# Chunk-selected attention and a top-1 expert layer on one core: a new written order, the last tile's down product in two column halves, and a first activation of one column

## The chip, the core and the metric

The kernel runs on one core of a Trainium2 chip. The metric is the device time of one execution in microseconds (us). TensorE is called PE, VectorE DVE, ScalarE ACT, GpSimd POOL and SyncE SP.

## The reference

```python
# attention: 4 batches, 8 heads, 768 positions, head size 64, float32
k_min, k_max = min and max of k over chunks of 32 positions            # 24 chunks
ub   = sum_d max(q_d * k_min_d, q_d * k_max_d)                         # bound for each query and chunk
sel  = the 6 chunks of highest ub among those not after the query's
attn = softmax(where(sel and causal, q @ k.T / 8, -1e9));  x = attn @ v   # x: 3072 tokens x 512
# expert layer: 8 experts, 512 -> 1024 -> 512, one expert for each token
p = softmax(x @ w_gate);  e = argmax(p)
out[token] = p[e] * (relu(x[token] @ w1[e]) @ w2[e])
```

## The kernel before, in words

The attention works on 16 pairs of heads, numbered 0 to 15, four to a batch. The two heads of a pair lie in the upper and lower 64 partitions. The routed tokens then go through the experts in 26 tiles, numbered 0 to 25, of 128 rows: tiles 0 to 9 hold tokens of the first three batches, so they can start before the last batch has been routed; tiles 10 to 25 wait for it. Tiles 20 to 25 share 128 rows between two experts.

All work is written as steps, such as `kt.12`: the step `kt` for pair 12. One long string, `ORDER`, lists every step of the program, and each engine and each queue runs its own steps in the order in which the string has them. An engine waits at a step until the data and the buffer are there, and everything behind that step on the same engine waits with it. The steps that matter here:

- `lk lq lv` load k, q and v of a pair (SP queue, L192, L194). `w.0` to `w.31` load and convert a quarter of one expert's weights each, 512 KB (POOL queue, L182).
- `kt qt` transpose k and q on PE (L208, tiles pk and pq). `kr0 kr1` reduce pk to chunk maxima and minima on DVE (L214). `qR qN` write the positive and negative part of q (ACT, L226), `kc qc` copy k and q to bf16 (ACT, L218 and L230).
- `ub` multiplies the bounds (PE, L242, tile pc). `sel1` to `selt` choose the chunks on DVE and end in the mask mt.
- `sc0` to `sc5` are six blocks of scores (PE, L288 and, for the mask, L296, tile ps), `ex0` to `ex5` their exponentials (ACT, L304), `cm` the causal corrections (POOL, L311), `av` the products with v (PE, L324, tiles ob and oa), `ac` the sums over blocks for the denominator (DVE, L335).
- `ocB ocA` copy the attention output from PSUM (ACT). `sm gt` (PE) and `uc` (ACT, L368) and `ut` (PE, tile pc, L199) and `rcp lgt` (DVE, L386 to L400) form denominators and gate logits. `xt` (PE, L199, tile px) and `xr` (DVE, L422) write the token rows. `lga` adds logits over pairs on POOL (L408).
- `ra` to `rp` route one batch, nearly all on DVE; `rx` is their one exponential, on ACT (L445), and `rk` their one product, on PE. `s0` to `s5` scatter a batch's rows to DRAM from POOL. `tA tB tC` compute on DVE the tables that say which rows and which expert a tile has.
- For a tile, `x` reads 128 token rows from DRAM through a DMA transpose (SP queue, L743), `U` is the product with w1 (PE, L783), `Rl` the relu (ACT, L792), `H` a DMA transpose of the hidden values (SP queue, L802), `D` the product with w2 (PE, L809), `Y` the scaling by the gate (ACT, L816), `O` the scatter to the output (POOL, L820). `g` fetches the tokens' gates and row numbers (ACT or POOL queue). `z` are matmuls on zeros at the start, `sp` pauses on POOL.

The PSUM tiles pk, pq, pc, ps, px and ph share three buffers. Which of the three a tile gets is fixed when the program is built, from the order in which the string gives and frees them; at run time PE waits until the last reader of the tile that had the buffer before is done. The hidden values h have two buffers, so `Rl` of a tile waits for the `H` of the tile two before.

The weights of all experts lie in two tiles, and a product picks its expert by a register; so the first `U` waits for all sixteen loads of w1, and the first `D` for all sixteen of w2. A `U` or `D` of a whole tile is 8 matmuls of 512 columns, or 16 where each half of the rows has its own expert; these come in pairs that use 64 columns of the array each.

## Time and profile before

| what | value |
|---|---|
| median of 3 runs | 308.94 us (308.81 to 317.49) |
| the profiled execution | 305.6 us, its span 303.7 us |
| PE busy | 285.2 us (94%) |
| DVE busy | 197.0 us (65%); next to nothing after 250 us |
| ACT, POOL busy | 189.3 us (62%), 159.5 us (53%) |
| granted TensorE clock | 0.998 of full speed |

Up to about 205 us the span is attention, with the first expert tile begun at 197.8 us; from there to 298 us it is the experts. An idle time in brackets stands behind an instruction that its engine began late, with what ended the wait; "issue" means that the profile shows no release. A matmul's end is modelled and reaches a little past the start of the next, so the distance from start to start is the better measure of what a group costs.

### The profile page before, as it was taken

Reading aid. Unit: us, or ns where it says so; the run is one execution under the profiler, and the core shown is the slowest. Engines: PE = TensorE matmul, PEld = TensorE weight load, DVE = VectorE, ACT = ScalarE, POOL = GpSimd, SP = SyncE. Lnnn points to the kernel's source line nnn. Section 1 sums busy time; section 2 is a strip of 40 time slices with the busy share of each in tenths; the row PEclk is TensorE's granted clock in tenths of the full one; section 3 lists DMA queues with packets and bytes.
Section 4 is the critical chain, followed back from the end, with each engine's and each line's share of the span. In section 5 each row is a group of like instructions: output and inputs, shape, how many; then the busy total and the mean of one; then the engine's idle time right before and its main releaser. Section 6 shows DMA issues by size and latency. Waiting matters only on the chain.

```text
span 303.7 us, 8579 instructions
## 1 busy us (share of the span) xinstructions
PE 285.2 (94%) x3095; PEld 145.3 (48%) x3105; DVE 197.0 (65%) x613; ACT 189.3 (62%) x266; POOL 159.5 (53%) x245
## 2 busy tenths in 40 slices
...
GB/s 152 201 193 202 201 190 210 177 204 167 208 163 160 191 208 211 149 229 171 189 244 204 159 205 194 106 167 149 224 224 176 208 150 210 235 191 228 139 172 77
DMA packets 132587, 56.51 MB, mean 186 GB/s; under 512 B 121915, under 2 KB 121917, under 8 KB 132544
## 3 DMA queue, kind: packets, MB, share of 16 engines
...
q14 instruction: 15, 0.12, 0.1%
HBM read 53.26 MB, written 9.99 MB: 208 GB/s over the span
## 4 chain that ended last, share of the span: by engine, by line
PE 61%; DVE 9%; issue 9%; POOL 6%; DMA 5%; ACT 4%; SPq 3%; POOLq 1%; DVEq 0%; ACTq 0%
PE oa L324 16%; PE ph L783 8%; PE py L809 6%; PE ps L288 6%; DVE Pa L335 5%; PE ps L296 5%; PE pc L242 4%; PE pc L352 4%; POOL out_dram L820 3%; PE ob L324 3%; PE pc L362 2%; DMA KQ<-xg 2%; PE pq L208 2%; PE px L199 2%; DMA x_early<-xs_dram 2%
## 5 line engine op out<-in xcount | busy, mean ns | idle before, releaser
L304 ACT ACTIVATE Pa<-ps 128x1024 f32<-128x1024 f32 x64 | 65.1, 1024 | 15.2 <-PE ps L296 10.0
L335 DVE TENSOR_TENSOR Pa<-Pa 128x1024 f32<-128x1024 f32 (+2 forms) x64 | 64.5, 1008 | 6.9 <-PE oa L324 2.2
L324 PE MATMUL oa<-Pa,v 128*64 128x512 f32 (+2 forms) x320 | 64.3, 518 | 0.0
L311 POOL TENSOR_SCALAR_AFFINE_SELECT Pa<-Pa 128x256 f32<-128x256 f32 x48 | 25.1, 538 | 50.0 <-ACT Pa L304 47.4
L809 PE MATMUL py<-w_all,hT 128*128 (+1 forms) x251 | 46.9, 379 | 1.5 <-issue 1.2
L792 ACT ACTIVATE h<-ph 128x1024 bf16<-128x1024 f32 (+1 forms) x27 | 26.5, 990 | 31.5 <-DMA hT<-h 12.7
L288 PE MATMUL ps<-KQ 64*128 64x512 bf16 (+3 forms) x256 | 37.3, 307 | 1.3 <-ACT Pa L304 0.6
L820 POOL DMA_INDIRECT out_dram<-y,tag_all x26 | 25.7, 989 | 22.9 <-ACT y L816 18.6
L500 POOL DMA_INDIRECT xs_dram<-xrow,sli x24 | 27.8, 1156 | 13.4 <-issue 4.8
L296 PE MATMUL ps<-mt,IND 64*128 64x256 bf16 (+4 forms) x512 | 34.4, 225 | 0.2 <-DVE mt L272 0.2
L809 PEld LDWEIGHTS <-hT 128*128 128x128 bf16 (+1 forms) x256 | 20.8, 102 | 26.0 <-issue 3.3
L816 ACT ACTIVATE y<-py,tag_all 128x512 f32<-128x512 f32 x26 | 17.6, 687 | 21.3 <-PE py L809 19.5
L214 DVE TENSOR_REDUCE KK<-pk 128x24 f32<-128x768 f32 x32 | 29.2, 943 | 1.3 <-PE pk L208 1.2
L324 PEld LDWEIGHTS oa<-Pa,v 128*64 128x64 f32 x320 | 19.4, 136 | 19.8 <-issue 14.7
L783 PE MATMUL ph<-w_all,x_early 128*128 (+1 forms) x125 | 25.3, 379 | 3.0 <-DMA x_early<-xs_dram 2.4
L288 PEld LDWEIGHTS <-KQ 64*128 64x128 bf16 x256 | 13.2, 94 | 28.9 <-issue 28.4
L296 PEld LDWEIGHTS <-IND 64*128 64x128 bf16 x512 | 23.0, 94 | 7.5 <-issue 0.4
L311 POOL TENSOR_SCALAR_AFFINE_SELECT Pb<-Pb 128x256 f32<-128x256 f32 x32 | 20.7, 672 | 9.7 <-ACT Pb L304 8.1
L182 POOL DMA_DIRECT2D w_all<-in_moe_w_dram x32 | 23.9, 748 | 0.1
L752 DVE TENSOR_TENSOR tag_all<-tag_all,inv_i 128x1 int32<-128x1 int32 x10 | 1.5, 158 | 31.8 <-DMA tag_all<-xs_dram 28.5
L783 PE MATMUL ph<-w_all,KQ 128*128 (+1 forms) x127 | 21.9, 380 | 0.1
L226 ACT ACTIVATE qN<-pq 128x576 f32<-128x576 f32 x16 | 10.4, 652 | 15.4 <-PE pq L208 15.4
...
## 6 DMA issues: line engine op xcount, KB each, us to landing
...
hT<-h SPq DMA_TRANSPOSE x27
out_dram<-y,tag_all POOLq DMA_INDIRECT x26
xs_dram<-xrow,sli POOLq DMA_INDIRECT x24
tag_all<-xs_dram ACTq DMA_DIRECT2D x20, 1.0 KB
```

The costliest lines, as they stand in the source:

```text
L214: nc.vector.tensor_reduce(KK[i % 2][:, n, 0:NCH], st[i]["pk"].rearrange("p (c w) -> p c w", w=CH), AX.X, ALU.max if n == 0 else ALU.min, n ...
L288: nc.tensor.matmul(ps[:, hd, ds(c0, w)], lhsT=kc_[r, ts(kb_, 128)], rhs=qc_[r, ds(q0, w)], start=True, stop=False, skip_group_check=True)
L296: nc.tensor.matmul(o[:, :, c, :], lhsT=IND[c][r, ts(kb_, 128)], rhs=mt[r, ds(j0, n), :], start=False, stop=True, skip_group_check=True)
L304: nc.scalar.activation(P[:], st[i][f"ps{u}"][:, :, 0:w], AF.Exp)
L311: nc.gpsimd.affine_select(out=pd, in_=pd, pattern=[[0, 2], [1, 128]], compare_op=ALU.is_ge, fill=0.0, base=0, channel_multiplier=-1)
L324: nc.tensor.matmul(po[64 * hd:64 * hd + 64, ds(q0 - o0, w)], lhsT=vt[:, kb_, hd, :], rhs=P[:, hd, ds(c0, w)], start=(u <= 1 and n == 0), s ...
L335: nc.vector.tensor_tensor(a[:, :, ds(q0_, w)], a[:, :, ds(q0_, w)], P[:, :, ds(c0, w)], ALU.add)
L500: d = nc.gpsimd.indirect_dma_start(out=xs_dram[:], out_offset=bass.IndirectOffsetOnAxis(ap=sli[:, u:u + 1], axis=0), in_=bst[b]["xrow"][:, ...
L783: nc.tensor.matmul(ph[r, fh, :], lhsT=fs[j]["xT"][:, c, r], rhs=w1_all[:, ds(wo + c * F + fh * 512, 512)], start=(c == 0), stop=(c == NDC ...
L792: nc.scalar.activation(h_[:, a].rearrange("q a (c j p) -> q (a c) j p", c=2, j=2), fs[j]["ph"][:, a].rearrange("q a (c p j) -> q (a c) j p ...
L809: nc.tensor.matmul(py[r], lhsT=fs[j]["hT"][:, c, r], rhs=w2_all[:, ds(wo + c * DM, DM)], start=(c == 0), stop=(c == NFC - 1), skip_group_c ...
L820: d = nc.gpsimd.indirect_dma_start(out=out[:], out_offset=bass.IndirectOffsetOnAxis(ap=tag_all[:, kind(j)[1], 1:2], axis=0), in_=fs[j]["y" ...
```

## The change

Three things change. A constant column `warm` is filled by an activation before all other work of ACT. The down product of tile 25, the last of those always run, is made in two halves of 256 columns, each in a PSUM bank of its own, and scaled by two activations instead of one; its scatter still comes after both. And the whole string `ORDER` is replaced by another order of the same steps.

```diff
+    warm = const.tile([128, 1], FP32)
+    nc.scalar.activation(warm[:], cbp[:], AF.Relu)
...
     def down_mm(j):
-        py = ps_o.tile([128, DM], FP32, tag=("oa", "ob")[j % 2], name="py")
-        for c in range(NFC):
-            for r, wo in fs[j]["gr"]:
-                nc.tensor.matmul(py[r], lhsT=fs[j]["hT"][:, c, r], rhs=w2_all[:, ds(wo + c * DM, DM)],
-                                 start=(c == 0), stop=(c == NFC - 1), skip_group_check=True)
-        fs[j]["py"] = py
+        if j == NS - 1:
+            ends = ps_s.tile([128, 2, 512], FP32, tag="s", name="py")
+            fs[j]["py"] = ends[:, :, 0:DM // 2]
+        else:
+            fs[j]["py"] = ps_o.tile([128, DM], FP32, tag=("oa", "ob")[j % 2], name="py")[:].unsqueeze(1)
+        n = fs[j]["py"].shape[2]
+        for a in range(DM // n):
+            for c in range(NFC):
+                for r, wo in fs[j]["gr"]:
+                    nc.tensor.matmul(fs[j]["py"][r, a], lhsT=fs[j]["hT"][:, c, r],
+                                     rhs=w2_all[:, ds(wo + c * DM + a * n, n)],
+                                     start=(c == 0), stop=(c == NFC - 1), skip_group_check=True)
...
-        nc.scalar.activation(y[:], fs[j]["py"][:], AF.Copy, bias=0.0, scale=tag_all[:, kind(j)[1], 0:1].bitcast(FP32))
+        n = fs[j]["py"].shape[2]
+        for a in range(DM // n):
+            nc.scalar.activation(y[:, ds(a * n, n)], fs[j]["py"][:, a], AF.Copy, bias=0.0,
+                                 scale=tag_all[:, kind(j)[1], 0:1].bitcast(FP32))
...
-        lk.0 lq.0 lq.1 lk.1 lv.0 lv.1 wg.0 kt.0 z.2 qt.0 kr0.0 qN.0 qR.0 kr1.0 z.3 ub.0 kc.0 qc.0 qt.1 sel1.0 selb.0
+        lk.0 lq.0 lq.1 lk.1 lv.0 kt.0 z.2 qt.0 lv.1 qR.0 kr1.0 qN.0 kr0.0 wg.0 z.3 ub.0 qc.0 sel1.0 kc.0 selb.0
```

In the middle of the attention PE's order stays nearly as it was: from pair 5 to pair 12 the string before has `qt kt av2 av3 av5 sc4 ub sc1 xt sm gt sc5 sc3 ut av1 sc2 sc0 av0 av4`, and the new one the same with `kt qt`. The following three places move further.

On SP's queue, where the attention's loads end and the expert tiles begin (`x_early` and `KQ` are targets of the step `x`, `hT` that of `H`), it was:

```order
L743 DMA_TRANSPOSE x_early<-xs_dram 128x4x128
L802 DMA_TRANSPOSE hT<-h 128x8x128
L743 ISA
L743 DMA_TRANSPOSE x_early<-xs_dram 128x4x128
L802 DMA_TRANSPOSE hT<-h 128x8x128 x2
L743 ISA
L743 DMA_TRANSPOSE x_early<-xs_dram 128x4x128
L743 ISA
L743 DMA_TRANSPOSE KQ_124<-xs_dram 128x4x128
```

and now it is, three lines of the file lower:

```order
L746 DMA_TRANSPOSE x_early<-xs_dram 128x4x128
L746 ISA
L746 DMA_TRANSPOSE x_early<-xs_dram 128x4x128
L746 ISA
L746 DMA_TRANSPOSE x_early<-xs_dram 128x4x128
L805 DMA_TRANSPOSE hT<-h 128x8x128
L746 ISA
L746 DMA_TRANSPOSE KQ_126<-xs_dram 128x4x128
L805 DMA_TRANSPOSE hT<-h 128x8x128
```

The first row of each piece is `x.3`. Before, `H.0`, `x.4`, `H.1` and `H.2` stood between it and the rest and `x.5` came after them; now `x.4` and `x.5` come first, and the `H` follow, with `x.6` and `x.7` between the first three. On PE the order there was `U.4 D.0 D.1 U.5 D.2` and is `U.4 D.0 U.5 D.1 D.2`.

On POOL, at the same place, the last weight loads (`w_all`, L182) and the last three additions of logits (`lg`, L408) stood so:

```order
L311 AFFINE_SELECT Pa<-Pa 128x2x128 x3
L182 DMA w_all<-in_moe_w_dram 128x2x1024
L408 TENSOR_TENSOR lg<-lg,lgt 128x96
L182 DMA w_all<-in_moe_w_dram 128x2x1024
L408 TENSOR_TENSOR lg<-lg,lgt 128x96 x2
L182 DMA w_all<-in_moe_w_dram 128x2x1024
L500 DMA xs_dram<-xrow,sli 24576x258 x3
```

and now:

```order
L411 TENSOR_TENSOR lg<-lg,lgt 128x96
L314 AFFINE_SELECT Pa<-Pa 128x2x128 x3
L314 AFFINE_SELECT Pc<-Pc 128x2x128
L185 DMA w_all<-in_moe_w_dram 128x2x1024 x2
L411 TENSOR_TENSOR lg<-lg,lgt 128x96 x2
L503 DMA xs_dram<-xrow,sli 24576x258 x3
```

The last weight load, a quarter of w2, stood behind the additions of pairs 14 and 15; now the last two loads stand ahead of both.

On ACT, in pair 9, the routing's exponential (`exl`) and the copy `ud` that PE's `ut.8` waits for stood so:

```order
L304 ACTIVATE Pa<-ps 128x1024
L445 ACTIVATE exl<-sh 128x48
L368 ACTIVATE ud<-pc 128x384
L304 ACTIVATE Pc<-ps 128x512
L304 ACTIVATE Pa<-ps 128x1024 x2
L304 ACTIVATE Pb<-ps 128x768
```

and now, from `uc.8` on:

```order
L448 ACTIVATE exl<-sh 128x48
L307 ACTIVATE Pc<-ps 128x512
L307 ACTIVATE Pa<-ps 128x1024 x2
L307 ACTIVATE Pb<-ps 128x768
L344 ACTIVATE ot<-ob 128x256
```

The copy `ud` (`uc.8`), which followed the exponential, now stands just ahead of it.

## Rows read from the trace of the kernel before

**Rows 1.** The page: busy us of each engine, share of the span, instructions.
```profile
PE 285.2 (94%) x3095; PEld 145.3 (48%) x3105; DVE 197.0 (65%) x613; ACT 189.3 (62%) x266; POOL 159.5 (53%) x245
```
**Rows 2.** Windows, `qt.10` to `qt.11` to `qt.12`: length, busy of each engine.
```profile
114.49:128.18 13.69, 12.31 (x173) 6.61 (x172) 11.84 (x36) 9.27 (x14) 8.94 (x12) 1.00 0.82 188
128.18:139.61 11.43, 11.43 (x161) 6.27 (x159) 10.37 (x31) 9.14 (x13) 5.57 (x11) 1.00 1.14 207
```
**Rows 3.** Windows, a stretch of the expert stage, same columns.
```profile
220.00:230.00 10.00, 9.95 (x47) 4.58 (x47) 0.00 (x0) 4.23 (x5) 6.39 (x9) 1.00 0.94 206
```
**Rows 4.** Timeline of PE: start, us, operation, idle before (`U.4`, `D.0`, `U.5`).
```profile
210.13 1.89 PE L783 MATMUL ph<-w_all,x_early 128*128 x8 [0.31 <-issue]
...
213.26 3.62 PE L809 MATMUL py<-w_all,hT 128*128 x15 [1.25 <-issue]
...
218.71 1.89 PE L783 MATMUL ph<-w_all,x_early 128*128 x8 [1.83 <-DMA x_early<-xs_dram]
```
**Rows 5.** Timeline of POOL there: last weight loads, and `lga.15` between them.
```profile
197.26 0.73 POOL L182 DMA_DIRECT2D w_all<-in_moe_w_dram  x1
...
205.09 0.39 POOL L408 TENSOR_TENSOR lg<-lg,lgt 128x96 f32<-128x96 f32 x1 [1.88 <-DVE lgt L400]
205.53 0.72 POOL L182 DMA_DIRECT2D w_all<-in_moe_w_dram  x1
```
**Rows 6.** Timeline of SP's queue there: `x.0` to `x.3`; `H.1`, `H.2`; `x.5`.
```profile
192.81 6.80 SPq L743 DMA_TRANSPOSE x_early<-xs_dram  x4
...
207.62 4.85 SPq L802 DMA_TRANSPOSE hT<-h  x2
212.63 1.19 SPq L743 DMA_TRANSPOSE x_early<-xs_dram  x1
```
**Rows 7.** Timeline of ACT there: `Rl.3`, which waits for `H.1` to land.
```profile
214.01 1.02 ACT L792 ACTIVATE h<-ph 128x1024 bf16<-128x1024 f32 x1 [5.09 <-DMA hT<-h]
```
**Rows 8.** Timelines of PE and DVE: `kt.6`, last `kr`, `ub.6`.
```profile
67.67 0.59 PE L208 MATMUL pk<-ident,k 64*128 64x64 f32 x12 [0.90 <-DVE xrow L422]
...
69.77 0.94 DVE L214 TENSOR_REDUCE KK<-pk 128x24 f32<-128x768 f32 x1
...
71.04 0.69 PE L242 MATMUL pc<-qR,KK 64*32 64x288 f32 x8
```
**Rows 9.** Timelines of ACT, PE and DVE: `uc.8`, `ut.8`, `rcp.8`.
```profile
123.35 0.49 ACT L368 ACTIVATE ud<-pc 128x384 f32<-128x384 f32 x1 [1.59 <-PE ps L296]
...
123.89 0.40 PE L199 MATMUL pc<-ident,ud 64*128 64x64 f32 x6 [1.04 <-issue]
...
124.40 0.27 DVE L386 RECIPROCAL rec<-pc 128x6 f32<-128x6 f32 x2 [0.79 <-PE pc L199]
```
**Rows 10.** Timelines of DVE and PE: `xr.8`, `sc3.10` in its buffer.
```profile
134.04 0.96 DVE L422 TENSOR_TENSOR xrow<-px,rec 128x768 bf16<-128x768 f32 x1
...
135.39 0.38 PE L288 MATMUL ps<-KQ 64*128 64x512 bf16 x2
```
**Rows 11.** Timelines of ACT and PE at the start: table load, `qR.0`, `ub.0`.
```profile
0.81 1.28 ACT L226 ACT_TABLE_LOAD   x1 [0.81 <-PEq L989]
...
8.17 0.65 ACT L226 ACTIVATE qR<-pq 128x576 f32<-128x576 f32 x1
...
8.91 0.69 PE L242 MATMUL pc<-qR,KK 64*32 64x288 f32 x8 [0.57 <-issue]
```
**Rows 12.** Timelines: `D.21` to `D.25`, `Y.25`, a mask product; group of `ocB`.
```profile
289.31 8.80 PE L809 MATMUL py<-w_all,hT 128*64 x80
...
298.20 0.69 ACT L816 ACTIVATE y<-py,tag_all 128x512 f32<-128x512 f32 x1 [1.04 <-PE py L809]
...
23.51 0.38 PE L296 MATMUL ps<-mt,IND 64*128 64x256 bf16 x4
...
23.82 0.45 PE L242 MATMUL pc<-qR,KK 64*32 64x288 f32 x4
...
L341 ACT ACTIVATE ot<-ob 128x256 f32<-128x256 f32 x16 | 6.4, 398 | 0.0
```

More of the change, by code (lines that the diff above doesn't have):

```diff
@@ new lines @@
+        xt.1 cm4.3 sc1.3 sm.2 w.13 ocA.2 xr.1 w.1 w.11 sel2b.4 gt.2 ex1.3 sc5.3 sel2a.4 sc3.3 sel3.4 ex5.3 av1.3
+        sc2.3 ex3.3 uc.2 selt.4 cm5.3 lq.5 ac4.3 sc0.4 av0.3 av4.3 ac5.3 ex2.3 ex0.4 lga.1 kt.5 qt.5 ac2.3 ocB.3
+        ut.2 rcp.2 kr0.5 cm3.3 qN.5 kr1.5 av2.3 qR.5 av3.3 qc.5 av5.3 lv.4 lgt.2 sc4.4 kc.5 ac3.3 cm0.4 ub.5 ac0.3
+        ex4.4 sel1.5 ocA.3 selb.5 lk.6 cm4.4 sc1.4 sm.3 sel2b.5 ex1.4 gt.3 uc.3 lq.6 sc5.4 sel2a.5 sc3.4 ut.3 sel3.5
+        ex5.4 av1.4 sc2.4 rcp.3 ex3.4 lga.2 xt.2 selt.5 cm5.4 lgt.3 lv.5 ac4.4 sc0.5 av0.4 av4.4 ac5.4 ex2.4 ex0.5
@@ new lines @@
+        kt.6 qt.6 lga.3 ac2.4 ocB.4 w.20 xr.2 kr0.6 cm3.4 qN.6 kr1.6 av2.4 qR.6 av3.4 qc.6 av5.4 sc4.5 kc.6 ac3.4
+        cm0.5 ub.6 ac0.4 ex4.5 sel1.6 ocA.4 selb.6 cm4.5 sc1.5 xt.3 xr.3 sm.4 sel2b.6 ex1.5 gt.4 uc.4 sc5.5 sel2a.6
+        sc3.5 ra.3 w.29 lq.7 rb.3 ut.4 sel3.6 ex5.5 av1.5 sc2.5 rc.3 rcp.4 ex3.5 lk.7 lv.6 selt.6 cm5.5 lgt.4 ac4.5
+        sc0.6 av0.5 w.12 av4.5 ac5.5 ex2.5 ex0.6 rd.3 rx.3 kt.7 qt.7 w.18 ac2.5 ocB.5 kr0.7 cm3.5 qN.7 kr1.7 av2.5
+        qR.7 av3.5 qc.7 av5.5 sc4.6 kc.7 ac3.5 lq.8 cm0.6 ub.7 ac0.5 ex4.6 sel1.7 ocA.5 selb.7 cm4.6 sc1.6 lk.8 xt.4
@@ new lines @@
+        xr.4 sm.5 sel2b.7 ex1.6 gt.5 uc.5 sc5.6 re.3 sel2a.7 sc3.6 rf.3 ut.5 sel3.7 ex5.6 av1.6 sc2.6 rcp.5 ex3.6
+        selt.7 cm5.6 lgt.5 ac4.6 sc0.7 av0.6 av4.6 ac5.6 ex2.6 ex0.7 w.0 lv.7 kt.8 qt.8 lga.5 lq.9 ac2.6 ocB.6 rk.3
+        kr0.8 cm3.6 qN.8 rm.3 kr1.8 av2.6 qR.8 av3.6 qc.8 av5.6 rn.3 sc4.7 kc.8 ac3.6 cm0.7 ro.3 ub.8 ac0.6 rp.3
+        ex4.7 lk.9 sel1.8 ocA.6 selb.8 w.6 cm4.7 sc1.7 xt.5 xr.5 sm.6 sel2b.8 ex1.7 gt.6 uc.6 sc5.7 sel2a.8 sc3.7
+        ut.6 sel3.8 ex5.7 av1.7 sc2.7 rcp.6 ex3.7 selt.8 cm5.7 lgt.6 ac4.7 sc0.8 av0.7 av4.7 ac5.7 ex2.7 ex0.8 kt.9
```

123 lines of the change are left out of this document (54 added, 69 removed).

## The prediction

> **What bounds the kernel now.** I read the page first: PE is busy for 285.2 of 303.7 us, so 18.5 us of the span are idle on PE [rows 1]. Next, the windows from one pair to the next. A pair without routing work takes 11.43 us, in which PE is busy throughout and DVE for 10.37; the pair before it, with routing steps between, took 13.69, with 12.31 and 11.84 [rows 2]. So PE sets the pace of the attention and DVE is close behind: where routing is added to a pair, DVE becomes the bound, and every wait that DVE or ACT passes on lengthens the pair. In the expert stage PE alone counts: 9.95 of 10 us [rows 3]. What a new order of the same work can win is therefore PE's idle time, found in PE's timeline. The last 5.6 us (the last `D` ends at 289.31 + 8.80 = 298.11, the span at 303.7) stay, since the last scatter follows them [rows 12]. Of the other 12.9 us, four waits make 5.0: `U.5` 1.83, `D.0` 1.25 [rows 4], `ut.8` 1.04 [rows 9] and `kt.6` 0.90 [rows 8]. The rest is small change and the start.
>
> **The change, part by part.** The sum is made against the profiled execution, 305.6 us (span 303.7 and 1.9 around it); the median of the timed runs, 308.94, stands 3.3 us above that, and I carry the difference over to it unchanged.
>
> *`U.5`.* It waits 1.83 us for `x.5` to land. `x.5` was issued at 212.63 [rows 6], although the rows it reads were there when `x.0` went out at 192.81: on SP's queue it stood behind `H.1` and `H.2`, which went out only from 207.62 on [rows 6]. In the new order `x.4` and `x.5` stand ahead of every `H`. Four loads took 6.80 us, 1.70 each [rows 6], so `x.5` leaves near 203 us, nine or ten earlier, while `U.5` is wanted at about 214. Minus 1.83.
>
> *`D.0`.* Its 1.25 us of idle have no releaser in the profile. The built program has its first matmul wait for weight loads; the last of them, a quarter of w2, was issued at 205.53, right behind `lga.15`, which waited 1.88 us for DVE [rows 5]. It would then have needed 7.7 us to land at 213.26. Now both last loads stand ahead of `lga.14` and `lga.15`, next to where the load of 197.26 stood [rows 5], eight us earlier. `D.0` also needs `H.0`, which now stands behind two more loads, 3.4 us; there is room for that, since `D.0` can't start before `U.4` ends, at about 212. Minus 1.25; bounds 0 and minus 1.25. What is late next is `H.1` for `D.1`: `H.1` was issued at 207.62 and its landing released `Rl.3` at 214.01 [rows 7], 6.4 us. The new PE order puts `U.5` ahead of `D.1`, which is then wanted at 212 + 2 x 1.75 = 215.5. So 1.5 us of room, and the two gains together are 3.1.
> After this PE runs without a gap [rows 3], so what is won here reaches the end.
>
> *`ut.8`.* It waited 1.04 us for `uc.8` on ACT, which began 1.59 us late behind `rx.7`, and DVE in turn waited 0.79 for `ut.8` [rows 9]. Now `uc.8` stands ahead of `rx.7`. DVE was idle there too, so most is kept: minus 0.8, the shorter of the two waits; bounds 0 and minus 1.04.
>
> *`kt.6`.* Its PSUM buffer came from `xr.2`, late on DVE. In the new program it waits for ACT's last exponential instead. But DVE is busy right there: the last `kr` of the pair ended at 69.77 + 0.94 = 70.71, and `ub.6`, which started at 71.04 [rows 8], would come to 70.14 and wait for it. So 0.33 to 0.90; since two routing steps have left this place, minus 0.4.
>
> *The start.* `ub.0` waited 0.57 us for `qR.0`, the second of ACT's steps [rows 11]. Now `qR` and `kr1` come first, which its first half needs. Against it `kc.0` moves behind `qc.0`, one copy of 0.7 us, and with it the buffer that the next transposes take. I take 0, bounds minus 0.57 and plus 0.7.
>
> *The column of ACT.* The table load already starts at 0.81 us and ends 5.5 us before ACT has anything to do; a one-column activation in that idle time costs and brings nothing: 0, bounds 0 and plus 0.65, the whole of `qR.0` [rows 11].
>
> *Tile 25.* The last five `D` are 80 matmuls in 8.80 us, 1.76 for one `D`: two 64-column halves run side by side, 220 ns a pair [rows 12]. In halves of 256 columns there are 16 pairs. At the same rate per column a pair takes 110 ns and nothing is lost. The nearest row with loads of weights for as short a stream is the mask product: four of 256 columns, two at a time, in 0.31 us (23.51 to 23.82 [rows 12]), 155 ns a pair, 2.48 in all. So 0 to plus 0.7; those weights are 128 columns wide, these 64, hence the middle, plus 0.36. `Y.25` shrinks from 0.69 to one of 256 columns, 0.40 by `ocB` [rows 12]: minus 0.29. Together plus 0.1.
> A rule speaks against this part: the Trainium skill, "TensorE: Matmul & The Clock Gate", sections "LDWEIGHTS (loading the stationary operand)" and "The mechanism", states that a load takes its columns / 1.2 in ns and overlaps running matmuls only if its rows differ. By it two loads of 64 columns, 107 ns, would be paid for every pair, and tile 25 would cost 1.7 us more, as an estimate, the sum ending at 306.3. The trace disagrees for these shapes: with 107 added to the streams the 80 matmuls would need nearly 13 us, not 8.80 [rows 12].
>
> *The rest of the attention.* PE's order per pair is the same but for `kt` and `qt`, and the routing steps are spread a little more evenly. Its idle time there, beyond the waits named, is under 8 us with the start (12.9 - 5.0). No row shows which of these waits stay: 0, bounds minus 4 (half of it) and plus 4.
>
> Sum: -1.83 - 1.25 - 0.8 - 0.4 + 0.1 = **-4.2 us**: 301.4 for a profiled execution, 304.7 for the median.
>
> **The rivals.**
> *A, the gain of the transition is taken back.* If hidden values land later than the 6.4 us of [rows 7], or `H.0` behind six loads is late, PE waits at `D.0` to `D.2` instead. For it: SP needed 4.85 us to issue `H.1` and `H.2` [rows 6]. Against it: 1.5 us of room. Then 1.83 and 1.25 are lost again: 307.8.
> *B, a new wait in every pair (slower).* The new pairs 5 to 12 repeat one pattern, so a wait that is sized wrongly is paid eight times. The place: `sc3` takes the buffer that `xr` frees. In a pair without routing `xr` ended at 135.00 and `sc3` began at 135.39 [rows 10], 0.39 us later; every routing step ahead of `xr` uses some of that up, and `rd.7` now stands ahead of `sel1.10`. The point from which it decides is an `xr` more than 0.39 later. The price is at most the 0.90 of `kt.6` [rows 8], also a wait for `xr`: 8 x 0.9 = 7.2, less 3.1 of the transition, 308.9 + 4.2 = 313; with A on top 316. Against it: routing steps stand so in few pairs, and the steps before `xr` have become fewer elsewhere.
> *C, the even spread works.* Half of the remaining 7.9 us is won as well: 304.7 - 3.9 = 300.8. For it: the 13.69 us pair against 11.43 [rows 2]. Against it: DVE's 11.84 us of work, at the density of the pair behind it (10.37 in 11.43), need 13.05 us [rows 2].
>
> **How the numbers follow.** Forecast 0.50 (304.7, its own range 302.5 to 306.5), A 0.22, C 0.14, B 0.14. The range 299.8 to 311.5 holds the forecast, A, most of C and the small cases of B. Two per cent, about what a measurement can tell from no change, is 302.8 or 315.1. Faster than that: most of C and the lower end of the forecast, 0.22. Slower: B with A, 0.07. Between: 0.71.
>
> **What would show it.** Right: no wait of PE at `U.5` and `D.0`; `x.5` issued before any `H`; the last `w_all` load near 197 us; `uc.8` directly behind `gt.8`; the last `D` at about 294 us and taking 1.8 to 2.5 us. Wrong: idle time of PE of 1 us or more at `D.0` to `D.2` with `hT` as its releaser (A); a wait of `sc3` for `xr` in several pairs in a row (B); or pairs 5 to 12 all near 11.5 us (C). It would be wrong altogether if the end of the attention moved by more than 4 us either way for a reason that no row here shows, such as the weight loads' new places slowing the loads of q, k and v.

## The result, and the profile after

The changed kernel is slower by 1.3%: a ratio of 1.0128, with a 95% interval from 1.0081 to 1.0175, written [1.0081, 1.0175] from here on. The medians are 309.93 us of six runs (308.17 to 318.06) and 308.07 us of six of the kernel before. Some executions of either kernel show a lower granted clock and a time some per cent longer; the ratios, here and below, leave them out. The forecast was 304.7, 1.4% faster. A second measurement, at the end of the experiments, gave 1.0056 [1.0009, 1.0103]. The profiled execution after took 308.17 us with a span of 306.2, before 305.6 with 303.7: 2.5 us of span to be found. Lines of the changed file are 3 higher up to the relu (L795 for L792); `D` is L818, `Y` L827, `O` L832.

The page's row of busy times answers to [rows 1]; PE's work is the same, so what is lost is idle time of PE or lies behind its last matmul.

```profile
PE 285.0 (93%) x3111; PEld 145.4 (47%) x3121; DVE 196.3 (64%) x613; ACT 190.2 (62%) x268; POOL 157.8 (52%) x245
```

**The transition** became quicker and later at once. First the windows of the kernel before, `x.0` issued to `U.0` to `U.6` (length, then busy time of each engine), then the same of after:

```profile
192.81:197.76 4.95, 4.38 (x53) 2.09 (x49) 3.49 (x8) 3.06 (x5) 3.48 (x7) 1.00 1.08 86
197.76:222.16 24.40, 20.61 (x152) 10.09 (x154) 15.96 (x68) 7.99 (x11) 10.99 (x15) 1.00 1.18 184
```

```profile
194.54:202.50 7.96, 5.48 (x60) 2.62 (x60) 6.02 (x13) 3.95 (x5) 4.61 (x7) 1.00 1.02 141
202.50:223.56 21.06, 20.15 (x150) 9.83 (x150) 14.80 (x67) 8.26 (x12) 7.07 (x10) 1.00 1.03 160
```

From `U.0` to `U.6` 3.34 us are won, about the 3.1 that were forecast for `U.5` and `D.0`. But `U.0` starts 4.74 later, 1.73 of it before `x.0` goes out and 3.01 between `x.0` and `U.0`. From `x.0` to `U.6` only 0.33 is left. PE's timeline there answers to [rows 4]: no wait at `D.0` (216.15), 0.56 at `U.5`.

```profile
202.50 1.90 PE L786 MATMUL ph<-w_all,x_early 128*128 x7
...
214.42 1.89 PE L786 MATMUL ph<-w_all,x_early 128*128 x8
216.15 1.67 PE L818 MATMUL py<-w_all,hT 128*128 x7
218.38 1.89 PE L786 MATMUL ph<-w_all,x_early 128*128 x8 [0.56 <-issue]
```

The 24.40 us of before are not typical of its order. In three further traces that have before's order at this place, the same stretch took 22.27 (`p1_parts`), 22.66 (`p5_uc`) and 22.25 us (`p16_before`), without a wait at `D.0` and with 0.82, 1.21 and 0.74 at `U.5`; a fourth (`p6_scatter`) took 23.54. PE of `p16_before`, `D.0` and `U.5`:

```profile
211.32 1.89 PE L809 MATMUL py<-w_all,hT 128*128 x8
...
216.26 1.89 PE L783 MATMUL ph<-w_all,x_early 128*128 x8 [0.74 <-DMA x_early<-xs_dram]
```

SP's queue and POOL's, for [rows 6] and [rows 5]: six `x` in a row before the first `H` (205.49), and the last two weight loads at 200.39. Before had three behind `x.0`, at 196.15, 197.26 and 205.53; after has these two, since its order brought one more ahead of `x.0`.

```profile
194.54 10.30 SPq L746 DMA_TRANSPOSE x_early<-xs_dram  x6
```

```profile
200.39 1.46 POOL L185 DMA_DIRECT2D w_all<-in_moe_w_dram  x2
```

**The attention** has new waits. PE's timeline, the instructions with the longest new or changed waits: `sc1.0`, `kt.2`, `ub.8`, `ut.8`, `ub.11`, the two at the end, and `U.8`:

```profile
13.69 0.39 PE L291 MATMUL ps<-KQ 64*128 64x512 bf16 x2 [0.81 <-ACT qR L229]
21.67 0.59 PE L211 MATMUL pk<-ident,k 64*128 64x64 f32 x12 [1.14 <-DMA k<-in_k_dram]
...
96.33 0.69 PE L245 MATMUL pc<-qR,KK 64*32 64x288 f32 x8 [0.82 <-ACT KQ L221]
...
125.69 0.40 PE L202 MATMUL pc<-ident,ud 64*128 64x64 f32 x6 [1.66 <-ACT ud L371]
...
134.28 0.69 PE L245 MATMUL pc<-qR,KK 64*32 64x288 f32 x8 [0.59 <-ACT KQ L221]
...
195.01 0.39 PE L291 MATMUL ps<-KQ 64*128 64x512 bf16 x2 [0.69 <-DVE lgt L403]
...
197.53 0.29 PE L291 MATMUL ps<-KQ 64*128 64x256 bf16 x2 [1.92 <-ACT Pa L307]
...
236.55 1.89 PE L786 MATMUL ph<-w_all,KQ 128*128 x8 [0.75 <-DVE sel L648]
```

Summed over all waits of 0.15 us or more, PE had lost 3.57 us by 23 us before and 5.12 after. This start did not stay behind: `ub.6` comes at 71.14 us against 71.04. From there after falls behind again, by 1.78 us at `ub.8`, 2.36 at `ub.11` and 2.28 at `ub.15`, and it loses most behind that. The last two rows of the attention, 2.61 us, stand where the kernel before had a single wait of 0.57. The windows from `ub.15` to `U.0`, before and then after:

```profile
179.60:197.76 18.16, 17.32 (x209) 8.71 (x205) 16.13 (x48) 11.52 (x16) 12.45 (x18) 1.00 0.95 152
```

```profile
181.88:202.50 20.62, 17.93 (x220) 9.23 (x221) 17.90 (x52) 11.73 (x16) 13.04 (x21) 1.00 1.00 178
```

The stretch grew by 2.46 us: PE's idle time in it from 0.84 to 2.69, and 0.61 of work that the new order puts behind `ub.15`.

**The end** grew by 0.88. PE, ACT and POOL of after, three views: `D.21` to `D.24` with the first tile-25 matmuls, the rest of tile 25, both halves of `Y.25`, the last scatter.

```profile
290.87 7.51 PE L818 MATMUL py<-w_all,hT 128*64 x72
298.71 1.50 PE L818 MATMUL py<-w_all,hT 128*64 128x256 bf16 x24 [0.32 <-SPq L968]
```

```profile
300.48 0.84 ACT L827 ACTIVATE y<-py,tag_all 128x256 f32<-128x256 f32 x2 [1.76 <-PE py L818]
```

```profile
301.60 0.97 POOL L832 DMA_INDIRECT out_dram<-y,tag_all  x1 [1.62 <-ACTq L968]
```

POOL's last scatter before:

```profile
299.16 0.97 POOL L820 DMA_INDIRECT out_dram<-y,tag_all  x1 [0.76 <-ACTq L956]
```

From the start of `D.21` to the last scatter: 9.85 before (289.31 [rows 12] to 299.16), 10.73 after (290.87 to 301.60). The sum closes: +1.73 to `x.0`, -0.33 to `U.6`, +0.16 to `D.21` (the 0.75 of `U.8` above against a wait of 0.58 before), +0.88 at the end, 2.4 of 2.5 us.

### The profile page after: what moved, and what is told of

It is laid out like the page before. It is cut to its first block, busy times and chain, and to the rows that moved or that the text cites. A ratio compares the mean times of both kernels' runs of the same rounds, so it can differ in the third digit from the quotient of the medians.

```text
span 306.2 us, 8598 instructions
## 1 busy us (share of the span) xinstructions
PE 285.0 (93%) x3111; PEld 145.4 (47%) x3121; DVE 196.3 (64%) x613; ACT 190.2 (62%) x268; POOL 157.8 (52%) x245
## 4 chain that ended last, share of the span: by engine, by line
PE 57%; DVE 14%; DMA 10%; issue 7%; ACT 4%; POOL 4%; SPq 2%; POOLq 0%; DVEq 0%; ACTq 0%
PE oa L327 13%; PE ph L786 10%; PE py L818 8%; DVE Pa L338 8%; PE ps L291 5%; PE ps L299 4%; PE pc L245 4%; DMA k<-in_k_dram 4%; PE pc L355 4%; DMA w_all<-in_moe_w_dram 3%; DVE KK L217 3%; POOL out_dram L832 3%; PE pc L365 2%; PE ob L327 2%; SPq L197 2%
## 5 line engine op out<-in xcount | busy, mean ns | idle before, releaser
L307 ACT ACTIVATE Pa<-ps 128x1024 f32<-128x1024 f32 x64 | 65.3, 1025 | 20.7 <-PE ps L299 13.1
L327 PE MATMUL oa<-Pa,v 128*64 128x512 f32 (+2 forms) x320 | 65.4, 519 | 0.2
L314 POOL TENSOR_SCALAR_AFFINE_SELECT Pa<-Pa 128x256 f32<-128x256 f32 x48 | 24.4, 524 | 49.9 <-ACT Pa L307 45.7
L818 PE MATMUL py<-w_all,hT 128*128 (+3 forms) x268 | 47.2, 367 | 0.5 <-SPq L968 0.3
L795 ACT ACTIVATE h<-ph 128x1024 bf16<-128x1024 f32 (+1 forms) x27 | 26.6, 991 | 27.4 <-PE ph L786 17.2
L832 POOL DMA_INDIRECT out_dram<-y,tag_all x26 | 25.7, 988 | 31.0 <-ACT y L827 16.9
L818 PEld LDWEIGHTS <-hT 128*128 128x128 bf16 (+1 forms) x272 | 21.5, 103 | 24.5 <-issue 1.7
L827 ACT ACTIVATE y<-py,tag_all 128x512 f32<-128x512 f32 (+1 forms) x27 | 18.0, 670 | 24.3 <-PE py L818 13.0
L314 POOL TENSOR_SCALAR_AFFINE_SELECT Pb<-Pb 128x256 f32<-128x256 f32 x32 | 18.9, 617 | 18.4 <-ACT Pb L307 18.4
L786 PE MATMUL ph<-w_all,KQ 128*64 (+1 forms) x126 | 22.3, 380 | 0.9 <-DVE sel L648 0.7
L221 ACT ACTIVATE KQ<-pk 128x768 bf16<-128x768 f32 x16 | 13.0, 814 | 8.1 <-DVE KK L217 6.5
```

The source lines that it names most:

```text
L307: nc.scalar.activation(P[:], st[i][f"ps{u}"][:, :, 0:w], AF.Exp)
L314: nc.gpsimd.affine_select(out=pd, in_=pd, pattern=[[0, 2], [1, 128]], compare_op=ALU.is_ge, fill=0.0, base=0, channel_multiplier=-1)
L327: nc.tensor.matmul(po[64 * hd:64 * hd + 64, ds(q0 - o0, w)], lhsT=vt[:, kb_, hd, :], rhs=P[:, hd, ds(c0, w)], start=(u <= 1 and n == 0), s ...
L786: nc.tensor.matmul(ph[r, fh, :], lhsT=fs[j]["xT"][:, c, r], rhs=w1_all[:, ds(wo + c * F + fh * 512, 512)], start=(c == 0), stop=(c == NDC ...
L795: nc.scalar.activation(h_[:, a].rearrange("q a (c j p) -> q (a c) j p", c=2, j=2), fs[j]["ph"][:, a].rearrange("q a (c p j) -> q (a c) j p ...
L818: nc.tensor.matmul(fs[j]["py"][r, a], lhsT=fs[j]["hT"][:, c, r], rhs=w2_all[:, ds(wo + c * DM + a * n, n)], start=(c == 0), stop=(c == NFC ...
```

## The experiments

Edits of the order are written as the steps around them; a line of three dots stands for what stays. "Before" and "after" are the two orders, "its code" the other two edits.

### The change in parts

`p1_parts`: the kernel before with the column and the halves.

```diff
-ORDER = after
+ORDER = before
```

> The order before, with only the two small parts of the change: the first column on ACT and tile 25 in two halves. Theory: the halves cost about 0.9 us at the end (the first half wants all eight parts of the hidden values within 0.9 us instead of 1.76 and waits about 0.6 us for the last ones to land; the two activations both start after the last matmul and take 0.15 us more than one), the column nothing: 0.9 us above the kernel before. Rival, as forecast: 0.1 us above it.

Median 308.25 against 306.63, 1.0038 [1.0001, 1.0075]; `D.21` to the last scatter took 10.63 us. So in this trace the halves cost 0.8 us, not 0.1, under the old order too.

`p11_noparts` is the converse, the kernel before with the new order alone.

```diff
-ORDER = before
+ORDER = after
```

> The kernel before with the new order alone: no column, tile 25 whole. Theory (the parts cost 0.9 us at the end and, since q of pair 0 landed 0.25 to 0.4 us later in the three runs with the column than in the two without, 0.3 us at the start): 1 to 1.3 us below the changed kernel, 1.2 to 1.5 us above the kernel before. Rival, as forecast: 0.1 us below the changed kernel.

1.0062 [1.0027, 1.0097]. The order by itself costs 0.3 to 1.0%. Of its trace, at a granted clock of 0.973, only the presence of waits is used: `ub.8` and `ub.11` with 0.82 each and one at the end of the attention, as in after; its last five `D` are 80 matmuls in 8.80 us, as before. One loss in it is not the changed kernel's: without the column ACT's table load starts at 8.12 us, not at 0.81, and `ub.0` waits 0.72.

### The transition

`p2_moves`: the transition's moves alone.

```diff
-lga.14 uc.15
+w.30 lga.14 uc.15
...
-rb.15 H.0
+rb.15 x.4 x.5 H.0
...
-rg.15 x.4 re.15
+rg.15 re.15
...
-rk.15 w.30 H.1
+rk.15 H.1
...
-rn.15 x.5 ro.15
+rn.15 ro.15
...
-D.0 H.3 D.1
+D.0 H.3 U.5 D.1
...
-sp.0 U.5 D.2
+sp.0 D.2
```

> The kernel before with four steps moved and nothing else: x.4 and x.5 ahead of H.0, the last weight load w.30 ahead of lga.14, U.5 ahead of D.1. Theory (the transition is what the change won): the waits of U.5 (1.83 us) and D.0 (1.25 us) go, 2.5 to 3.1 us below the kernel before. Rival: the hidden values become late instead, PE waits 1 us or more at D.0 to D.2, and the time stays within 1 us of the kernel before.

1.003 [0.9989, 1.0071]: nothing gained. SP's queue and PE of `p2_moves`:

```profile
193.00 12.42 SPq L743 DMA_TRANSPOSE x_early<-xs_dram  x6
```

```profile
209.99 1.89 PE L783 MATMUL ph<-w_all,x_early 128*128 x8 [1.97 <-DMA x_early<-xs_dram]
```

The waits at `D.0` and `U.5` are gone, and `U.3` waits 1.97 us instead. Six `x` took 12.42 us, 2.07 each, where the prediction had put 1.70 for each. The place on SP's queue was not the limit here; the transfer was.

`p3_splice`: after's code with before's order up to `x.0` and after's from there.

```diff
-ORDER = after
+ORDER = before up to x.0, then what is left, as after has it
```

> The changed kernel, with the order of the kernel before up to the first x (about 192 us) and the new order from there on. Theory (the loss is made before 200 us, in the attention): 2 us below the kernel before, since the new order after 205 us has 2.3 us less idle time on PE and the halves cost some of it. Rival (the transition wins only because the attention before it came late, and it would wait again here): within 1 us of the kernel before.

1.004 [1.0004, 1.0076]. `U.0` starts at 198.87, 3.6 us earlier than in after, and then PE waits 1.44 for `x`, 0.44 for a relu and 0.69 for `x` again: 23.67 us from `U.0` to `U.6`. Less the 0.8 of the halves, 0.3%, little is left between it and the kernel before. So the order from `x.0` on does not make the stretch short by itself. Two things that after has are missing here: its `U.0` comes 7.96 us after `x.0`, not 4.96, so that the rows have landed, and it has two weight loads behind `x.0`, not three. This run does not tell them apart; `p14_two` below does.

`p7_weights` and `p8_weights_x` put the last three weight loads ahead of `x.0`, the second with the moves of `p2_moves` as well.

```diff
-cm0.15 av1.15
+cm0.15 w.26 w.14 w.30 av1.15
...
-x.0 w.26 av2.15
+x.0 av2.15
...
-ac2.15 w.14 Rl.0
+ac2.15 Rl.0
...
-rk.15 w.30 H.1
+rk.15 H.1
```

> The kernel before with the last three weight loads (w.26, w.14, w.30, issued at 196, 197 and 205.5 us) issued together behind cm0.15, at about 190 to 193 us, where the DMA engines are less busy (share 0.78 against 1.23 from 195 to 210 us). Theory: the loads of token rows for the first expert tiles take less than 1.7 us each, D.0's wait of 1.25 us goes and part of U.5's 1.83 us; 1 to 2 us below the kernel before. Rival (the transposing loads set the pace by themselves): U.5 waits as before, and only D.0's wait may go; within 0.7 us of the kernel before.

> The same, and x.4, x.5 ahead of H.0 and U.5 ahead of D.1 besides. In the run with these x moves alone six loads took 12.4 us, and PE waited 1.97 us at U.3 instead of at D.0 and U.5. Theory (weight loads were what made them slow): six loads take 9 us or less, no wait of over 0.5 us at U.3 to D.2, and the time is 2.5 to 3 us below the kernel before. Rival (the transposing loads set the pace by themselves): six loads take 12 us again, U.3 waits 1.5 us or more, and the time stays within 1 us of the kernel before.

1.0309 [1.0264, 1.0354] and 1.0236 [1.0181, 1.0292]: a miss, and the clearest run of the study. POOL and PE of `p7_weights`, then the window of its `U.0`:

```profile
193.71 2.19 POOL L182 DMA_DIRECT2D w_all<-in_moe_w_dram  x3
```

```profile
208.87 3.57 PE L783 MATMUL ph<-w_all,x_early 128*128 x8 [7.44 <-DMA x_early<-xs_dram]
```

```profile
208.87:211.00 2.13, 2.13 (x6) 0.73 (x6) 0.00 (x0) 0.00 (x0) 0.00 (x0) 0.50 0.00 0
```

Three loads of 512 KB issued just ahead of `x.0` hold `U.0` for 7.44 us, by an estimate 2.5 us a load. So token rows wait behind weights on the DMA engines, not on SP's queue. After the idle time PE ran at a granted clock of 0.50, the lower level of 1.2 GHz, and the 8 matmuls took 3.57 us, not 1.89.

Next, loads moved far ahead, into a stretch with less traffic: `p9_gap` moves two, `p10_gap_x` adds the moves of `p2_moves`, `p13_one` and `p14_two` move one, or two with the second elsewhere, always with those moves.

```diff
# p9_gap, p10_gap_x
-w.22 ex4.7
+w.22 w.14 ex4.7
...
-w.23 qR.11
+w.23 w.30 qR.11
...
-ac2.15 w.14 Rl.0
+ac2.15 Rl.0
...
-rk.15 w.30 H.1
+rk.15 H.1
# p13_one: w.30 alone; p14_two: w.30, and w.14 behind w.0
```

> The kernel before with two weight loads moved far ahead, to where its DMA engines stood nearly idle: w.30 (205.5 us) behind w.23 (126.6 us; DMA share 0.03 from 126 to 128 us), w.14 (197.3 us) behind w.22 (91.3 us; share 0.55 from 90 to 92 us). Theory (the loads of token rows queue behind weight loads on the DMA engines; three loads put just ahead of them held U.0 up by 7.4 us, 2.5 us for each load): D.0's wait of 1.25 us goes, the first four loads of rows are issued in under 6.8 us, and U.5 waits under 1.83 us; 1 to 2.5 us below the kernel before. Rival (the transposing loads set the pace by themselves): U.5 still waits and the time stays within 0.7 us of the kernel before.

> The same, with x.4 and x.5 ahead of H.0 and U.5 ahead of D.1. Theory: now the six loads take 10 us or less instead of 12.4, and the waits from U.1 to D.2 sum to under 1 us; 2.5 to 3 us below the kernel before. Rival: U.3 waits about 2 us again, as with the x moves alone, and the time stays within 1 us of the kernel before.

> The kernel before with one weight load moved far ahead (w.30, issued at 205.5 us, behind w.23 at 126.6, where the DMA engines stood idle) and the three x moves (x.4, x.5 ahead of H.0, U.5 ahead of D.1). Theory: w.14's place near 91 us is what made q of pair 9 late in the run with two moved loads (1.47 and 0.54 us); without that move those waits stay under 0.3 us, U.0 to the first matmul of U.6 takes 21 to 22.5 us instead of 24.4, and the time is 2 to 3 us below the kernel before. Rival: one load less in front of the rows of tokens is too little, U.3 waits 1 us or more, and the time stays within 1 us of the kernel before.

> The same, and w.14 (197.3 us) behind w.0 (172 us). Theory: 0.5 us or so better than with one load moved, since the two loads at 196 and 197 us were what the first rows of tokens met: U.0 to U.6 in 21 us, 2.5 to 3.5 us below the kernel before. Rival: at 172 us it makes k or q of pair 15 late by up to 2.5 us, one load's time, and the gain is gone.

Ratios 1.0069 [1.0029, 1.0108], 1.0011 [0.9979, 1.0043], 1.0012 [0.9979, 1.0045] and 1.0019 [0.9983, 1.0056]. Without the moves (`p9_gap`) `U.5` still waits 1.25 us. With a load out of the way and the moves, `U.0` to `U.6` takes 20.85, 21.01 and 20.92 us; the window of `p10_gap_x`, PE busy for 20.29 of it:

```profile
200.93:221.78 20.85, 20.29 (x153) 10.01 (x152) 15.26 (x65) 7.61 (x10) 6.87 (x9) 1.00 0.88 150
```

Against the 24.40 of the first trace of before that is the forecast's 3 us; against the 22.25 of `p16_before`, on the chip of `p13_one` and `p14_two`, it is 1.2 to 1.3. It needs both the moves and a load less, and no late `U.0`: in `p14_two` `U.0` stands 5.04 us after `x.0`, as in before (4.95). So a load less is enough for the short stretch, and after has only two behind `x.0`, as has `p13_one`. But the bytes have to pass somewhere. PE of `p10_gap_x`, where q and k of pair 9 are late behind the new place of one load, as in `p9_gap` and in no run without that move; then of `p13_one`, behind the new place of the other load, which went out at 127.09:

```profile
105.04 0.59 PE L208 MATMUL pq<-ident,q 64*128 64x64 f32 x12 [1.47 <-DMA q<-in_q_dram]
106.16 0.91 PE L208 MATMUL pk<-ident,k 64*128 64x64 f32 x12 [0.54 <-DMA k<-in_k_dram]
```

```profile
137.86 0.39 PE L288 MATMUL ps<-KQ 64*128 64x512 bf16 x2 [1.04 <-DVE xrow L422]
...
143.18 0.59 PE L208 MATMUL pk<-ident,k 64*128 64x64 f32 x12 [0.54 <-DMA k<-in_k_dram]
```

The same two waits are in `p14_two`, 1.14 and 0.61. These sums, 1.6 to 2.0 us, are of the size of what the transition wins, and the time of the three runs is that of the kernel before to within 0.6%. That it is one for one is not shown. Waits of 1 to 2 us for q or k also come without any move: in `p13_one` q of pair 10 waits 2.13 us at 116.05, eleven us before the moved load goes out, and in `p16_before` k of pair 14 waits 1.50.

### The end of the attention

`p15_end`: the kernel before with after's order up to `ub.15`, and before's from there.

```diff
-ORDER = before
+ORDER = after up to ub.15, then what is left, as before has it
```

`p18_v` is that with two weight loads moved down, which in `p15_end` stood ahead of v of the last pair.

```diff
-qc.15 w.27 w.23 tA.0
+qc.15 tA.0
...
-s3.11 sc5.14
+s3.11 w.23 sc5.14
...
-s5.11 tA.1
+s5.11 w.27 tA.1
```

> The new order up to the bounds of pair 15 (about 182 us) and from there the order of the kernel before; tile 25 whole, no column. Theory (the end of the new attention and its quick transition are one and the same time, seen twice: U.0 comes 8 us after x.0 instead of 5, and the rows of tokens have landed meanwhile): the waits of 0.7 and 1.9 us before U.0 become 0.6 to 1.5 us, but U.1 to D.2 wait 1.5 to 3 us again, and the start of U.6 and the end stay within 0.8 us of the new order alone, that is 1.5 to 2.5 us above the kernel before. Rival (two separate things): both are won, and it comes within 0.5 us of the kernel before or below it.

> The new order to pair 15 and the old one from there, as in the run before this, with two weight loads (w.23, w.27, issued at 177 us ahead of v of pair 15) moved behind the scatters s3.11 and s5.11. Theory (v of pair 15 landed 13 us after its issue because three weight loads stood ahead of it): its waits of 1.40 and 0.33 us go, and the time is 1 to 1.7 us below that run, 0.5 to 1.2 us above the kernel before. Rival (the two loads now stand ahead of the rows of tokens instead): U.0 or U.1 waits 1 to 3 us, no gain.

1.0073 [1.0034, 1.0111] and 1.0049 [1.0011, 1.0088]. In `p15_end` `U.0` to `U.6` takes 21.25 us, but v of pair 15 is late; in `p18_v` v is in time and a `U` waits. PE of `p15_end`, then of `p18_v`:

```profile
191.69 1.04 PE L324 MATMUL oa<-Pa,v 128*64 128x512 f32 x2 [1.40 <-DMA v<-in_v_dram]
```

```profile
212.75 3.17 PE L783 MATMUL ph<-w_all,x_early 128*128 x8 [2.41 <-issue]
```

Both are no better than after's order as a whole (`p11_noparts`, 1.0062). The reason given for `p15_end` failed: the transition stays quick with the old order around it, so it does not need after's late end. Again the loads come into it. `p15_end` has two weight loads behind `x.0`, like after, and three just ahead of v (176.33), and v is late; `p18_v` moves two of these down, to 181.40 and 189.31, and there relus wait 1.45 and 2.17 us for hidden values and then `U.4` 2.41. What the end of the attention would cost with the loads at their old places, no run shows.

### `ut.8`

`p5_uc` moves `uc.8` ahead of `rx.7`; `p6_scatter` takes two of the scatters of routed rows, `s2.3` and `s3.3`, from beside it. Both are single runs, for their traces.

```diff
# p5_uc
-gt.8 rx.7 sc5.9 sc3.9 uc.8 ex5.9
+gt.8 uc.8 rx.7 sc5.9 sc3.9 ex5.9
# p6_scatter
-kr0.10 s2.3 av5.8
+kr0.10 av5.8
...
-sm.8 s3.3 xr.7
+sm.8 xr.7
...
-cm3.9 ac2.9
+cm3.9 s2.3 s3.3 ac2.9
```

> The kernel before with one step moved: uc.8 ahead of rx.7 on ACT, as in the changed kernel. The forecast's reason: uc.8 is late because it stands behind rx.7, so ut.8 waits 0.2 us or less instead of 1.04. Theory now: PE's own semaphore updates come late there (in the changed kernel gt.8's update came 1.85 us after the end of its last matmul, in the kernel before 1.23 us), while POOL issues two scatters of token rows in a row; the place of rx.7 plays no part, and ut.8 still waits 0.8 us or more.

> The kernel before with two steps moved on POOL: the scatters s2.3 and s3.3 stand one pair later, behind cm3.9. Theory: with no scatter beside gt.8 its update comes within 0.1 us of the end, uc.8 starts 0.7 us after gt.8 instead of 1.9, and ut.8's wait of 1.04 us is gone; the late updates move to where the two scatters now are (about 126 to 129 us). Rival (something in the pair itself, such as rx.7 or the pace of DVE): the wait stays at 0.8 us or more.

ACT and PE of `p5_uc`, for [rows 9]:

```profile
123.50 0.49 ACT L368 ACTIVATE ud<-pc 128x384 f32<-128x384 f32 x1 [1.70 <-PE ps L296]
```

```profile
124.05 0.40 PE L199 MATMUL pc<-ident,ud 64*128 64x64 f32 x6 [1.02 <-issue]
```

`rx.7` is no longer ahead of `uc.8`, and `ut.8` waits 1.02 us as before: the step's reason was wrong. In `p6_scatter`, with one scatter left beside `gt.8`, the wait is 0.29. What makes `uc.8` late is seen in after, PE (`gt.8`), ACT (`uc.8`) and POOL (the two scatters):

```profile
122.64 0.63 PE L365 MATMUL pc<-ot,wgb 128*32 128x128 f32 x8
```

```profile
125.15 0.49 ACT L371 ACTIVATE ud<-pc 128x384 f32<-128x384 f32 x1 [2.76 <-PE ps L299]
```

```profile
122.31 0.99 POOL L503 DMA_INDIRECT xs_dram<-xrow,sli  x1 [0.17 <-DVE ubm L258]
123.61 0.98 POOL L503 DMA_INDIRECT xs_dram<-xrow,sli  x1 [0.30 <-issue]
```

`gt.8` ended at 123.27, and ACT was released 1.88 us later, 0.56 after the end of the second scatter. Moving the scatters has a price of its own: they free the row buffer that `xr.8` writes, and `p6_scatter`, which took 310.37 us, has this wait on PE:

```profile
138.55 0.39 PE L288 MATMUL ps<-KQ 64*128 64x512 bf16 x2 [2.80 <-DVE xrow L422]
```

`p5_uc` took 304.19 us, less than the fastest run of the kernel before in the same batch (304.58, median 306.49); a single run does not show whether the move wins anything.

### The start

`p4_start` gives after the order of before up to `kt.3`; `p12_k2` puts `lk.2` back ahead of `lq.2`.

```diff
# p4_start
-ORDER = after
+ORDER = before up to kt.3, then what is left, as after has it
# p12_k2 (of after)
-ac2.0 lq.2
+ac2.0 lk.2 lq.2
...
-sel1.1 lk.2
+sel1.1
```

> The changed kernel, with the order of the kernel before up to the transpose of pair 3's keys (about 35 us) and the new order from there on. Theory: the 1.7 us of idle time that PE gained in the first 23 us (1.14 us for k of pair 2 alone) go, and the end comes 1.5 to 2 us earlier than in the changed kernel, about 0.8 us above the kernel before. Rival: DVE is the bound of the pairs with routing, takes the gain up again by pair 11, and the time stays that of the changed kernel, 2.5 us above the kernel before.

> The changed kernel with one step moved: lk.2 ahead of lq.2 on SP, as in the kernel before. Theory: k of pair 2 lands some 2 us earlier and kt.2's wait of 1.14 us goes to 0.3 or less, and as PE bounds the pairs behind it, the start of ub.3 to ub.5 comes about 1 us earlier and the end 0.5 to 1.1 us below the changed kernel. Rival (DVE or the order of loads takes it back): ub.5 and the end come as in the changed kernel.

`p4_start` failed as an experiment: the two orders have their loads at different places, and the splice put k of pair 4 so late that PE waited 6.76 us for it; 1.04 [1.0348, 1.0452] says nothing of the start. `p12_k2` is 1.0114 [1.0064, 1.0164], no better than after. Its trace, at a granted clock of 0.979, has no wait for k and a longer one for q, on PE:

```profile
21.82 0.59 PE L211 MATMUL pq<-ident,q 64*128 64x64 f32 x12 [3.98 <-DMA q<-in_q_dram]
```

### Both kernels once more, on another chip

`p16_before` and `p17_after` are the two kernels with no edit at all, run one after the other.

> The kernel before unchanged, for its trace on the same chip as the changed kernel. Theory: as in the first trace of it; where no semaphore update of PE comes late beside a scatter (as on two of the chips so far), ut.8 does not wait and x.0 is issued 1 to 2 us earlier than on a chip where they do.

> The changed kernel unchanged, on the same chip. Theory: slower than before by 1.0 to 1.3%, and the difference in place: about 0.8 us after the start of D.21 (10.6 to 10.7 us to the last scatter instead of 9.85), the waits of ub.8, ub.11 and the end of the attention, 2.5 to 4 us, before U.0, and 3 us given back between U.0 and U.6. Rival: on this chip the attention is not slower, and only the tail's 0.8 us (0.3%) stays.

1.0056 [1.0009, 1.0103], spans 301.3 and 302.9. ACT of `p17_after`: `uc.8` starts 0.04 us after `gt.8`, whose row is the same as in after to the last digit (122.64, 0.63), with a scatter beside it (122.34) as there:

```profile
123.31 0.49 ACT L371 ACTIVATE ud<-pc 128x384 f32<-128x384 f32 x1 [0.90 <-PE pc L365]
```

`ut.8` does not wait there, in either kernel. Most other waits of after are there again: `kt.2` 1.45, `sc1.0` 0.81, `ub.8` 0.81, `ub.11` 0.84, the end of the attention 1.49, `U.8` 1.00. `U.0` is 2.23 us later than in `p16_before` and `U.0` to `U.6` 1.25 shorter (21.00 against 22.25). From `ub.15` to `U.0` this pair differs by 2.49 us (20.39 against 17.90), as the first did by 2.46: it is the one loss that both pairs of traces show alike. The tail, expected at 10.6 to 10.7 us, took 10.03. Here too the sum closes: +2.23 to `U.0`, -1.25 to `U.6`, +0.41 to `D.21`, +0.17 at the end, 1.6 of 1.6 us.

## Why the prediction was wrong

Two steps of the sum failed most: the 0 for the rest of the attention, where the new order loses time up to `U.0` (4.74 us in the first pair of traces, 2.23 in the second), and the -3.1 for `U.5` and `D.0`, which had the wrong cause and was sized on one trace. `ut.8` and tile 25 add to it.

**`U.5` and `D.0`, -3.1.** The waits went nearly as said, and 3.3 us of the stretch from `U.0` with them; in the second pair of traces only 1.25, since in three of four other traces of before's order `D.0` did not wait and in all four `U.5` waited 0.74 to 1.21. The step failed in its cause. It read a late issue on SP's queue, and a late weight load on POOL's, as questions of order; `p2_moves` shows that the same moves alone win nothing, `p7_weights` that a load of 512 KB ahead of the rows costs by an estimate 2.5 us, and `p10_gap_x` that the stretch becomes short where a load is taken out of it, at the price of 1.5 us at q and 0.5 at k. After took one out too, which the prediction did not see. The DMA share was in the rows that I had read: 0.94 in [rows 3], 1.14 in [rows 2]. I used the 1.70 us of an `x` from [rows 6] as if it were the instruction's own time; an `x` took 1.19 there by itself, and 2.07 in `p2_moves`. Rival A was right in kind, that the gain of the transition is taken back, but `p2_moves` shows it by the token rows and not the hidden values, and its 307.8, 0.4% below the kernel before, was not reached.

**`ut.8`, -0.8.** It measured +0.6 (1.66 against 1.04), and in the second pair 0. `uc.8` was not held by `rx.7` (`p5_uc`) but by a late signal from PE beside two scatters. The name of the releaser, PE, stood in [rows 9]; I took it for the engine that the order had put ahead.

**The rest of the attention, 0, and the start, 0.** Here most of the loss lies, and most of that behind `ub.15`. By 23 us after had lost 1.55 us more than before, outside the bounds of the start (+0.7), but by `ub.6` it was made up. `sc1.0` waits for a buffer behind `qR`, a sort of wait that the step had priced. `kt.2` waits too, and its cause is open: `lq.2` now stands ahead of `lk.2`, but turned round q is late instead (`p12_k2`), and in the three runs of the new order without the column (`p11_noparts`, `p15_end`, `p18_v`) `kt.2` does not wait. In pairs 8 and 11 PE waits, through ACT's `kc`, for DVE. The window of after's pair 8 has DVE busy for 12.13 of 12.91 us; below it are ACT's `kc.8`, which waits 1.20 us for DVE's second reduction, and DVE's order there:

```profile
83.42:96.33 12.91, 12.09 (x176) 6.60 (x170) 12.13 (x32) 9.71 (x15) 4.48 (x9) 1.00 1.03 200
```

```profile
95.47 0.81 ACT L221 ACTIVATE KQ<-pk 128x768 bf16<-128x768 f32 x1 [1.20 <-DVE KK L217]
```

```profile
93.51 0.94 DVE L217 TENSOR_REDUCE KK<-pk 128x24 f32<-128x768 f32 x1
94.38 0.19 DVE L487 TENSOR_TENSOR rk<-pr,base_e 128x48 f32<-128x48 f32 x1
94.50 0.94 DVE L217 TENSOR_REDUCE KK<-pk 128x24 f32<-128x768 f32 x1
```

The same pair before took 12.02 us with DVE busy for 11.55, and had no wait. So rival B was right in kind, a routing step ahead of something that PE waits for, and wrong in place (`kc` and `ub`, not `xr` and `sc3`) and in number: it was paid at two pairs, 0.8 and 0.6, not at eight. At the end of the attention ACT's exponential waited 4.90 us for a sum over blocks, which stood behind the tables on DVE; ACT of after:

```profile
196.46 1.02 ACT L307 ACTIVATE Pa<-ps 128x1024 f32<-128x1024 f32 x1 [4.90 <-DVE Pa L338]
```

That holds `U.0` back. Before had the tables on DVE there too, and an exponential waited 1.49 us for a sum. The step had bounds of 4 us either way, because no row showed which waits would stay; the new ones are these.

**Tile 25, +0.1.** The mis-sized term: +0.88, +0.8 in `p1_parts`, +0.2 in `p17_after`. The rate was right: in `p17_after`, where nothing is waited for, `D.21` to `D.25` took 8.82 us, in whole tiles 8.80 [rows 12]; less four `D` of 1.76 that is 1.78 for tile 25, 111 ns a pair against the 110 forecast. So no load of weights was paid; the 107 ns a pair that the prediction worked out by the Trainium skill, "TensorE: Matmul & The Clock Gate", section "LDWEIGHTS (loading the stationary operand)", are not seen. Three other things were left out, of which the rows of after give the sizes. The first half uses all eight parts of the hidden values in half the time, and PE catches up with their transfer: 0.32 us idle, and 0.54 more in all from `D.21` to the last matmul's end (300.21 - 290.87 against 8.80). ACT is released 0.27 us after that end, where it was 0.09 [rows 12]. And both `Y` start only then, so that the overlap behind the -0.29 does not take place: two activations take 0.84, one took 0.69. Together 0.87 of the 0.88; in `p17_after` without the first two it is 0.2 (10.03 against 9.85).

**`kt.6`, -0.4,** was right: the wait for `xr.2` is gone and `ub.6` starts at 71.14 us, as in [rows 8] within 0.1 in spite of the start. **The column, 0,** came out for a reason that holds only in the old order. It is done at 2.30, long before ACT's first work at 8.05; ACT of after:

```profile
0.81 1.28 ACT L92 ACT_TABLE_LOAD   x1 [0.81 <-PEq L1001]
2.10 0.20 ACT L92 ACTIVATE warm<-cbp 128x1 f32<-128x1 f32 x1
```

In the new order without the column the table load does not start at 0.81 but at 8.12 (`p11_noparts`), 7.38 (`p15_end`) and 7.70 (`p18_v`), just ahead of `qR.0`, and `ub.0` waits behind both; PE of `p15_end`:

```profile
9.42 0.69 PE L242 MATMUL pc<-qR,KK 64*32 64x288 f32 x8 [1.36 <-issue]
```

So the column belongs to the new order: it keeps the load early. What it is worth in the whole time is not shown, since `kt.2` waits in after and `p17_after` and not in these three runs.

Two slips in the prediction's sums, 4.2 for 7.2 less 3.1 in rival B and "nearly 13" for 13.1 in tile 25, change nothing. The measured time lies inside the range; the sign of the forecast was wrong. No version that ran more than once is faster than the kernel before: `p10_gap_x` and `p13_one` are equal to it to within half a per cent. What stays open: how much of the order's loss each of the small waits makes up, since they shift one another, and what the order would take with every weight load at its old place.
